# A gated-attention recurrence whose operands are prepared one chunk ahead in every round, instead of a lead that grows to two

## The chip, the cores and the metric

The kernel runs on one core of one Trainium2 chip. The metric is the device time of one execution in microseconds; the time before is 1066.51 us, the median of three runs.

## The reference, cut to what matters

Three stages follow each other: a gated linear attention over 4 batches of 768 tokens with 8 heads of 48, a mixture of 8 experts with the best two for each token, and a gated feed-forward layer with root-mean-square norm. The change lies in the first.

```
f = 1 / (1 + exp(-f_logit))
state = 0
for t in range(S):                       # 768 steps, every batch and head by itself
    state = f[t, :, None] * state + outer(k[t], v[t])
    y[t]  = q[t] @ state
x = y                                    # as (3072, 384)
noisy = x @ w_gate + log1p(exp(x @ w_noise)) * noise     # the router: two best of 8 experts
out += w * (relu(x[mask] @ w1[e]) @ w2[e])               # for each expert and each of the two
...                                                      # then norm, silu(gate) * val, w_out
```

## The kernel before

The recurrence is worked off in chunks of 128 tokens: 4 batches of 6 chunks, 24 chunks (numbers 0 to 23), all 8 heads of a chunk at once as 4 pairs in 128 partitions. With c the running sum of the gates' logarithms inside a chunk, the keys are scaled by exp(c) and the queries by exp(-c), so that a chunk needs only plain products.

What a chunk n passes through, by function:

- `clip` (L333, ACT): bounds the gate logits in place in `Fs`. `gates` (L343, ACT): two activations, exp and ln, into `L`, which has 2 buffers. `sums` (L351, DVE): a running sum over `L` into `cs`, which has 4 buffers; it is what frees a buffer of `L`.
- `prep` (L368): four steps. ACT makes `Ek` from `cs`, DVE the scaled keys `KT`, ACT turns `cs` over, DVE makes the scaled queries `QT` (and POOL copies a column to `hs`, for a check at the end). `KT` and `QT` have 3 buffers.
- `keys` (L387): PE transposes `KT`, ACT copies the result to `Ks`. The last chunk of a batch (5, 11, 17, 23) has no `keys` and no `state`.
- `scores` (L402): PE multiplies keys and queries; `masks` (L414, DVE) writes the masked product `AM`.
- `inter` (L447, PE): queries times the carried state, left out in the first chunk of a batch (0, 6, 12, 18). `state` (L421, PE) and `carry` (L433, DVE, tiles `su` and `Ss`) advance the state.
- `attend` (L458): PE adds `AM` times values, ACT copies the sum to `yT`. `rows` (L472): PE turns it into token rows and router logits, ACT copies out `x`, DVE reduces the logits to `lg`.

One round i of the loop in `gla_stream` (L1108) handles chunk i, finishes `rows` of chunk i-1 and prepares later chunks. The order of work on PE, ACT, DVE and POOL is written out: each of these engines executes its instructions in the order in which the program issues them, so that an instruction that waits holds up everything behind it on its engine. SP issues the plain loads and stores, in an order that a planner makes.

The lead before: `due(i, grows, lead)` (L1174) says which chunks a step of round i handles. Up to round `grows` it is chunk i+lead; in round `grows` two chunks at once; from then on chunk i+lead+1. Clips double in round 2, gates in round 3, sums in round 4, preps in round 5. From round 6 on the keys and queries of chunk i+2 are made in round i, and `keys(i+1)` stands right behind the first step of `prep`; in rounds 1 to 5 (`short`) it stands behind `inter(i)`. The loads of keys and queries (`load_kq_after`) and of gate logits (`load_f_after`) are issued behind the `prep` and `gates` of odd chunks, for the pair of chunks whose buffers these free.

Other work is spread over the rounds. `safe()` is called three times in a round (behind `scores`, behind `inter` and at the end) and each time takes one piece from the list `routing`: in rounds 12 to 19 the steps of the router for the first 12 chunks (mostly DVE, a few matmuls), from round 19 on the row gathers for the first expert blocks. In rounds 20 to 23 `take_part` splits a piece of expert weights into a high and a low part (ACT `whi`, DVE `wlo`), and in rounds 22 and 23 the first expert block's rows are transposed. After the loop the experts and the feed-forward layer follow as one stream of matmuls, again in an order written out for PE; the other engines' order is there made by the planner.

Of the kernel before, what the change touches and what calls it, by code (L numbers as in the profile page):

```python
# [27 lines left out]
def tile_gated_attention_moe_ffn(  # L28
# [23 lines left out]
    NT = B * NCH  # L52
# [100 lines left out]
    def bank(use, i=None):  # L153
        b = banks[0][use]
        if i is None:
            i = turns[use] = turns.get(use, -1) + 1
        k_ = b[i % len(b)]
        return (late["pp"] if k_ in "12" else pp).tile([P, 512], F32, name="bank" + k_)
# [141 lines left out]
    def load_f(n, count=2, cuts=WHOLE):  # L300
        b, src, dst = chunks_of(n, count)
        t = Fs[n // 2 % 3]
        for s in cuts:
            nc.sync.dma_start(t[:, s, dst], f_logit[b, s, :, src].rearrange("a d t -> d a t"))
        for k_ in range(count):
            _, _, at_ = chunks_of(n + k_, 1)
            st["f", n + k_] = t[:, :, at_]
# [13 lines left out]
    def load_f_after(n):  # L321
        if n % 2 and n + 5 < NT:
            load_f(n + 5)

    def load_kq_after(n):
        if n % 2 and n + 5 < NT:
            load_kq(n + 5)

    def run(fn, n, cuts=WHOLE):
        for _ in zip(*[fn(n, s) for s in cuts]):  # L330
            pass

    def clip(n, s=slice(0, HP), scalar=True):  # L333


        f = st["f", n][:, s]
        st["shift", n] = scalar
        if scalar:
            nc.scalar.activation(f, f, AF.Relu, bias=shift)
        else:  # L340
            nc.vector.tensor_scalar(f, f, -GATES_MAX - 1.5, None, op0=OP.max)

    def gates(n, s=slice(0, HP)):  # L343

        if s.start == 0:
            st["L", n] = wk.tile([P, HP, P], F32, name="L")
        f, l = st["f", n][:, s], st["L", n][:, s]
        nc.scalar.activation(l, f, AF.Exp, scale=-1.0, bias=shift if st["shift", n] else 0.0)
        nc.scalar.activation(l, l, AF.Ln, bias=1.0)

    def sums(n, s=slice(0, HP)):  # L351

        if s.start == 0:
            st["cs", n] = wk.tile([P, HP, P], F32, name="cs", bufs=4)
        nc.vector.tensor_tensor_scan(st["cs", n][:, s].rearrange("p a t -> p (a t)"),  # L355
                                     chain[:, s].rearrange("p a t -> p (a t)"),
                                     st["L", n][:, s].rearrange("p a t -> p (a t)"), 0.0,
                                     op0=OP.mult, op1=OP.add)
# [9 lines left out]
    def prep(n, s=slice(0, HP)):  # L368

        if s.start == 0:  # L370
            st["KT", n] = wk.tile([P, HP, P], F32, name="KT", bufs=3)
            st["QT", n] = wk.tile([P, HP, P], F32, name="QT", bufs=3)
            st["Ek", n] = wk.tile([P, HP, P], F32, name="Ek", bufs=1)
        cs, Ek = st["cs", n][:, s], st["Ek", n][:, s]
        nc.scalar.activation(Ek, cs, AF.Exp)
        yield
        nc.vector.scalar_tensor_tensor(st["KT", n][:, s], Ek, KEYS_MAX, st["kq", n][:, s, 0],
                                       op0=OP.min, op1=OP.mult)
        yield
        nc.scalar.activation(cs, cs, AF.Exp, scale=-1.0)  # L380
        yield
        nc.vector.tensor_tensor(st["QT", n][:, s], cs, st["kq", n][:, s, 1], op=OP.mult)
        if s.stop == HP:
            nc.gpsimd.tensor_copy(hs[:, n], st["cs", n][:, :, P - 1])
        yield

    def keys(n, copy=True):  # L387

        if n % NCH == NCH - 1:
            return  # L390
        p = cut(bank("K"), HP, P)
        for a in range(HP):
            flip(p[:, a, :], st["KT", n][:, a, :], ident)
        st["pK", n] = p
        if copy:
            keys_out(n)
# [711 lines left out]
    def gla_stream():  # L1108
        def valid(n):
            return 0 <= n < NT  # L1110

        with tc.manual_schedule(engines=ALL):
            rest = constants()
            load_f(0, 1, PARTS)
            next(rest)
            warm(10)
            load_kq(0, 1)
            load_f(1, 1)
            load_v(0)
            load_kq(1, 1)  # L1120
            load_f(2)
            load_kq(2)
            load_v(1)
            load_f(4)
            load_v(2)
            nc.sync.dma_start(columns[:, :, NX:], moe_w_both[:, :, :2 * E])
            load_kq(4)
            load_v(3)
            for t in Vs:
                nc.gpsimd.memset(t[:, DM:], 0.0)  # L1130
            for t in Ks + Ss:
                nc.gpsimd.memset(t[:, :, D:], 0.0)
            run(decay, 0, PARTS)
            halves = [prep(0, s) for s in PARTS]
            for _ in range(2):
                for half in halves:
                    next(half)
            clip(1, scalar=False)
            for _ in range(2):
                for half in halves:  # L1140
                    next(half)
            warm(3)
            keys(0, copy=False)
            gates(1)
            keys_out(0)
            scores(0, masked=False)
            sums(1)
            clip(2, scalar=False)
            masks(0)
            warm(2)  # L1150
            state(0)
            more = prep(1)
            next(more)
            next(more)
            next(rest)
            next(more)
            gates(2)
            next(more)
            carry(0)
            warm(5)  # L1160
            inter(0)
            attend(0)
            sums(2)
            keys(1)
            clip(3, scalar=False)
            gates(3)
            clip(4, scalar=False)
            next(rest)
            load_f_after(1)
            load_f_after(3)  # L1170
            load_kq_after(1)


            def due(i, grows, lead):  # L1174

                if i < grows:
                    ns = (i + lead,)
                elif i == grows:
                    ns = (i + lead, i + lead + 1)
                else:  # L1180
                    ns = (i + lead + 1,)
                return [n for n in ns if n < NT]

            for i in range(1, NT + 2):
                routing.extend(plan.get(i, []))
                if valid(i + 3):
                    load_v(i + 3)
                if valid(i):
                    scores(i)
                safe()  # L1190
                short = i < 6
                preps = due(i, 5, 1)
                more = prep(preps[0]) if preps else iter(())
                next(more, None)
                if valid(i + 1) and not short:
                    keys(i + 1)
                next(more, None)
                next(more, None)
                if valid(i - 1):
                    rows(i - 1)  # L1200
                for fn in turning.get(i, []):
                    fn()
                if valid(i):
                    inter(i)
                if valid(i + 1) and short:
                    keys(i + 1)
                safe()
                next(more, None)
                for n in preps[1:]:
                    run(prep, n)  # L1210
                for n in preps:
                    load_kq_after(n)
                if valid(i):
                    state(i)
                    carry(i)
                for n in due(i, 3, 3):
                    gates(n)
                    load_f_after(n)
                if valid(i):
                    attend(i)  # L1220
                for n in due(i, 4, 2):
                    sums(n)
                for n in due(i, 2, 4):
                    clip(n)
                safe()
                if i == 4:
                    nc.sync.dma_start(noise, moe_noise)
                    nc.sync.dma_start(gcol, moe2_rms_g)
                if i in (14, 16):
                    start_loads()  # L1230
                if i == 18:
                    nc.sync.dma_start(yd.rearrange("(e s) d -> s e d", e=E)[min(CAPS):],
                                      zeros[:, None, :].to_broadcast([SPAN - min(CAPS), E, DM]))
                if 20 <= i < 24:
                    take_part(0)
# [280 lines left out]
```

## Time and profile before

| what | value |
|---|---|
| time, median of 3 runs | 1066.51 us (1062.62 to 1069.57) |
| the profiled execution's own time | 1063.08 us |
| its span, first to last instruction | 1061.3 us |
| PE busy | 1027.7 us, 97% |
| DVE busy | 674.1 us, 64% |
| ACT busy | 486.1 us, 46% |
| POOL busy | 307.5 us, 29% |
| mean granted TensorE clock | 0.99 |

Busy shares are means over the whole span. The recurrence takes up its first part, some 150 us; in the rest PE hardly stops. A busy PE is not a PE at full clock: the granted clock stands in a column of its own.

### The profile page before, as it was taken

The numbers are of one execution on the slowest core, as the hardware profiler recorded it, in microseconds if no ns is written. First come the engines' busy times: TensorE is split into PE (matmuls) and PEld (weight loads), VectorE is DVE, ScalarE is ACT, GpSimd is POOL, SyncE is SP. The second block draws the span as 40 slices with busy tenths as digits, with TensorE's granted clock in tenths as the row PEclk, the third lists the DMA queues.
The fourth block names the chain that finished last, engine by engine and source line by source line (L and its number), as shares of the span: only waits on it lengthen the run. The fifth ranks groups of instructions, "written<-read, shape, count | busy, mean of one in ns | idle before, by whom it ended". The sixth has DMA issues, their size and how long they took to land.

```text
span 1061.3 us, 17487 instructions
## 1 busy us (share of the span) xinstructions
PE 1027.7 (97%) x6449; PEld 938.4 (88%) x6449; DVE 674.1 (64%) x1521; ACT 486.1 (46%) x1054; POOL 307.5 (29%) x350
## 2 busy tenths in 40 slices
PE   8998899999999999999999999999999999999996
PEld 5787789999999999999999988888888888888885
DVE  7698979878777757876665796354353354453332
ACT  6696655655555544655555543223232232232221
POOL 2000145545556655555550250110110200200000
PEclk9799999999999999999999999999999999999999
DMA  9975345666677756545555340110110200200000
GB/s 303 313 259 176 120 129 184 218 195 208 219 244 236 220 166 205 179 143 173 180 165 155 121 127 1 48 43 1 60 31 1 68 22 1 75 16 1 31 1 33
DMA packets 88946, 134.45 MB, mean 127 GB/s; under 512 B 8703, under 2 KB 64915, under 8 KB 88851
## 3 DMA queue, kind: packets, MB, share of 16 engines
q1 hardware_dynamic: 79475, 113.82, 32.7%
q0 software_dynamic: 9376, 19.43, 6.6%
q8 instruction: 52, 0.85, 0.3%
q14 instruction: 43, 0.35, 0.1%
HBM read 107.63 MB, written 25.59 MB: 126 GB/s over the span
## 4 chain that ended last, share of the span: by engine, by line
PE 77%; DVE 9%; DMA 7%; ACT 3%; issue 3%; SPq 1%; DVEq 0%; ACTq 0%
PE bank L681 68%; DMA raw<-in_moe_w_dram 5%; PE bank L173 2%; PE bank L476 2%; PE bank L454 2%; DVE wlo L210 1%; PE bank L464 1%; PE scores L408 1%; ACT whi L209 1%; DVE cs L355 1%; PE bank L725 1%; PE bank L728 1%; DVE AM L418 1%; PE bank L429 1%; DVE hh L816 1%
## 5 line engine op out<-in xcount | busy, mean ns | idle before, releaser
L681 PE MATMUL bank<-whi,hh 128*128 128x384 f32 x1360 | 379.7, 336 | 0.2 <-DVE y L843 0.2
L681 PE MATMUL bank<-xhi,whi 128*128 128x512 f32 (+8 forms) x816 | 303.3, 372 | 3.9 <-DVE hh L816 3.7
L681 PE MATMUL bank<-xhi,wlo 128*128 128x512 f32 (+8 forms) x816 | 301.3, 369 | 0.0
L681 PE MATMUL bank<-xlo,whi 128*128 128x512 f32 (+8 forms) x816 | 300.9, 369 | 0.0
L681 PEld LDWEIGHTS bank<-whi,hh 128*128 128x128 f32 x1360 | 248.5, 187 | 3.9 <-DVE y L843 0.6
L681 PE MATMUL bank<-wlo,hh 128*128 128x384 f32 x680 | 228.0, 335 | 0.0
L681 PEld LDWEIGHTS bank<-xhi,whi 128*128 128x128 f32 x816 | 153.3, 188 | 26.1 <-DVE hh L816 7.5
L681 PEld LDWEIGHTS bank<-xhi,wlo 128*128 128x128 f32 x816 | 153.2, 188 | 18.7 <-issue 0.2
L681 PEld LDWEIGHTS bank<-xlo,whi 128*128 128x128 f32 x816 | 153.3, 188 | 16.2
L210 DVE TENSOR_TENSOR wlo<-raw,whi 128x256 fp32r<-128x256 f32 (+1 forms) x320 | 143.1, 485 | 24.7 <-ACT whi L209 17.2
L209 ACT ACTIVATE whi<-raw 128x256 fp32r<-128x256 f32 (+1 forms) x320 | 126.2, 451 | 44.5 <-DMA raw<-in_moe_w_dram 33.0
L782 POOL DMA_INDIRECT xg<-xd,stokr x107 | 108.5, 1014 | 76.6 <-ACT hh L819 45.0
L681 PEld LDWEIGHTS bank<-wlo,hh 128*128 128x128 f32 x680 | 127.5, 187 | 3.3
L919 DVE TENSOR_TENSOR sg<-bank,sg 128x512 f32<-128x512 f32 x72 | 49.7, 691 | 120.2 <-ACT sg L918 120.2
L816 DVE SCALAR_TENSOR_TENSOR hh<-bank,hh 128x384 fp32r<-128x384 f32 (+7 forms) x176 | 76.4, 455 | 77.3 <-ACT hh L819 72.8
L870 POOL DMA_INDIRECT xg<-yd,slots x40 | 43.8, 1094 | 265.3 <-ACT hh L922 254.9
L782 POOL DMA_INDIRECT xg<-xd,stoka x84 | 90.3, 1075 | 89.9 <-ACT hh L819 56.9
L819 ACT ACTIVATE hh<-bank 128x384 fp32r<-128x384 f32 (+7 forms) x128 | 64.0, 500 | 103.0 <-PE bank L681 69.6
L918 ACT ACTIVATE sg<-bank 128x512 f32<-128x512 f32 x72 | 42.9, 596 | 143.3 <-PE bank L681 134.6
L922 ACT ACTIVATE hh<-sg 128x512 fp32r<-128x512 f32 x72 | 45.4, 630 | 123.7 <-DVE sg L920 123.6
L923 DVE TENSOR_TENSOR hh<-sg,hh 128x512 fp32r<-128x512 f32 x72 | 50.9, 706 | 46.8 <-ACT hh L922 46.8
L920 DVE TENSOR_TENSOR sg<-bank,sg 128x512 f32<-128x512 f32 x72 | 49.7, 691 | 40.2 <-PE bank L681 39.9
(172 smaller groups left out, 1003.2 us busy)
## 6 DMA issues: line engine op xcount, KB each, us to landing
raw<-in_moe_w_dram SPq DMA_DIRECT2D x64, 768.0 KB
Qs<-in_kq_dram SPq DMA_DIRECT2D x11, 1024.0 KB
yd<-y SPq DMA_DIRECT2D x48, 192.0 KB
Fs<-in_f_logit_dram SPq DMA_DIRECT2D x11, 512.0 KB
Vs<-in_v_dram SPq DMA_DIRECT2D x24, 192.0 KB
xd<-x SPq DMA_DIRECT2D x24, 192.0 KB
ya<-y SPq DMA_DIRECT2D x24, 192.0 KB
raw<-in_moe_w_gate_dram SPq DMA_DIRECT2D x6, 768.0 KB
```

The source lines that it names most:

```text
L209: nc.scalar.activation(hi[:, j], raw[:, j], AF.Copy)
L210: nc.vector.tensor_tensor(lo[:, j], raw[:, j], hi[:, j].bitcast(F32), op=OP.subtract)
L681: nc.tensor.matmul(o, a, b, start=start and i == 0, stop=stop and i == 2)
L782: paced(nc.gpsimd.indirect_dma_start(out=b.xg[i][:, k_], out_offset=None, in_=table, in_offset=bass.IndirectOffsetOnAxis(ap=rows_of[:, k_, ...
L816: return nc.vector.scalar_tensor_tensor(o, p[:, c], 0.0, hh[:, 0, c].bitcast(F32), op0=OP.max, op1=OP.subtract).ins
L819: mark[0] = nc.scalar.activation(hh[:, 0, :N], p[:, :N], AF.Relu).ins
L870: paced(nc.gpsimd.indirect_dma_start(out=y, out_offset=None, in_=ya if n < GROUP else yd, in_offset=bass.IndirectOffsetOnAxis(ap=at_, axis ...
L918: nc.scalar.activation(sg, ps[0], AF.Sigmoid)
L919: nc.vector.tensor_tensor(sg, ps[0], sg, op=OP.mult)
L920: nc.vector.tensor_tensor(sg, ps[1], sg, op=OP.mult)
L922: mark[0] = nc.scalar.activation(hh[:, 0], sg, AF.Copy).ins
L923: mark[1] = nc.vector.tensor_tensor(hh[:, 1], sg, hh[:, 0].bitcast(F32), op=OP.subtract).ins
```

## The change

The growing lead is taken out. `due` goes, and every round i prepares chunk i+1 (`prep`, `keys`), sums chunk i+2, takes the gates of chunk i+3 and clips chunk i+4. `keys(i+1)` stands behind `inter(i)` in all rounds. No computation is added or removed over the 24 chunks; it is dealt out to other rounds. Rounds 0 and 1 are as they were.

```
-            def due(i, grows, lead):
-                if i < grows:
-                    ns = (i + lead,)
-                elif i == grows:
-                    ns = (i + lead, i + lead + 1)
-                else:
-                    ns = (i + lead + 1,)
-                return [n for n in ns if n < NT]
-
             for i in range(1, NT + 2):
...
-                short = i < 6
-                preps = due(i, 5, 1)
-                more = prep(preps[0]) if preps else iter(())
+                more = prep(i + 1) if valid(i + 1) else iter(())
                 next(more, None)
-                if valid(i + 1) and not short:
-                    keys(i + 1)
                 next(more, None)
                 next(more, None)
                 if valid(i - 1):
                     rows(i - 1)
...
                 if valid(i):
                     inter(i)
-                if valid(i + 1) and short:
+                if valid(i + 1):
                     keys(i + 1)
                 safe()
                 next(more, None)
-                for n in preps[1:]:
-                    run(prep, n)
-                for n in preps:
-                    load_kq_after(n)
+                if valid(i + 1):
+                    load_kq_after(i + 1)
                 if valid(i):
                     state(i)
                     carry(i)
-                for n in due(i, 3, 3):
-                    gates(n)
-                    load_f_after(n)
+                if valid(i + 3):
+                    gates(i + 3)
+                    load_f_after(i + 3)
+                if valid(i + 4):
+                    clip(i + 4)
                 if valid(i):
                     attend(i)
-                for n in due(i, 4, 2):
-                    sums(n)
-                for n in due(i, 2, 4):
-                    clip(n)
+                if valid(i + 2):
+                    sums(i + 2)
                 safe()
```

## Rows read from the trace of the kernel before

**Rows 1.** Stretches: length; PE, PEld, DVE, ACT, POOL busy; granted clock, DMA share, GB/s.

```profile
16.00:21.40 5.40, 4.15 (x61) 3.56 (x62) 4.19 (x11) 3.92 (x8) 0.66 (x1) 1.00 1.11 345
36.10:49.90 13.80, 13.65 (x111) 11.48 (x109) 7.87 (x12) 6.88 (x14) 0.37 (x2) 0.51 0.92 326
64.60:69.70 5.10, 5.10 (x80) 4.53 (x78) 4.52 (x8) 4.30 (x8) 0.22 (x1) 1.00 0.64 211
97.60:101.10 3.50, 3.50 (x46) 3.15 (x43) 2.91 (x15) 2.29 (x5) 0.19 (x1) 0.52 0.16 59
```

**Rows 2.** Instructions in time around round 4: start, us, engine, idle before and releaser.

```profile
33.27 0.72 ACT L348 ACTIVATE L<-Fs,shift 128x512 f32<-128x512 f32 x1 [0.77 <-DVE cs L355]
34.56 0.58 ACT L469 ACTIVATE yT<-bank 128x512 f32<-128x512 f32 x1
35.19 1.15 PE L476 MATMUL bank<-columns,yT 128*128 128x112 f32 x8 [1.91 <-ACT yT L469]
```

**Rows 3.** The same view of round 2, PE and DVE: lead of one.

```profile
22.60 1.22 DVE L418 TENSOR_TENSOR AM<-scores,mask 128x1024 f32<-128x1024 f32 x1
23.75 0.68 DVE L377 SCALAR_TENSOR_TENSOR KT<-Ek,Qs 128x512 f32<-128x512 f32 x1
24.58 0.66 PE L173 MATMUL bank<-ident,KT 128*128 128x128 f32 x4
25.17 0.67 PE L429 MATMUL bank<-Vs,Ks 128*64 128x48 f32 x16
25.67 1.06 PE L464 MATMUL bank<-AM,Vs 128*64 128x128 f32 x16
25.89 0.36 DVE L442 TENSOR_TENSOR su<-bank,Ss 128x192 f32<-128x192 f32 x1 [0.70 <-PE bank L429]
27.87 1.23 DVE L418 TENSOR_TENSOR AM<-scores,mask 128x1024 f32<-128x1024 f32 x1
```

**Rows 4.** The same view, masks of rounds 6, 12, 14, 15, 17, 18, 20, 23.

```profile
51.69 1.20 DVE L418 TENSOR_TENSOR AM<-scores,mask 128x1024 f32<-128x1024 f32 x1
...
80.11 1.23 DVE L418 TENSOR_TENSOR AM<-scores,mask 128x1024 f32<-128x1024 f32 x1 [0.65 <-PE scores L408]
...
94.37 1.21 DVE L418 TENSOR_TENSOR AM<-scores,mask 128x1024 f32<-128x1024 f32 x1
...
103.00 1.20 DVE L418 TENSOR_TENSOR AM<-scores,mask 128x1024 f32<-128x1024 f32 x1
...
116.14 1.20 DVE L418 TENSOR_TENSOR AM<-scores,mask 128x1024 f32<-128x1024 f32 x1
...
122.05 1.20 DVE L418 TENSOR_TENSOR AM<-scores,mask 128x1024 f32<-128x1024 f32 x1
...
131.39 1.20 DVE L418 TENSOR_TENSOR AM<-scores,mask 128x1024 f32<-128x1024 f32 x1
...
146.83 1.22 DVE L418 TENSOR_TENSOR AM<-scores,mask 128x1024 f32<-128x1024 f32 x1
```

**Rows 5.** The same view, pieces of router and weight work inside the rounds.

```profile
97.28 0.20 PE L537 MATMUL bank<-r_both,before 128*128 128x96 bf16 x1 [3.94 <-DVE r_both L534]
98.35 0.26 DVE L544 COPY r_pos<-bank 128x104 f32<-128x104 f32 x1
110.68 1.22 DVE L575 TENSOR_TENSOR r_ol<-irowh,r_hf 128x1024 f16<-128x1024 f16 x1
113.01 0.69 DVE L377 SCALAR_TENSOR_TENSOR KT<-Ek,Qs 128x512 f32<-128x512 f32 x1
121.76 0.78 PE L585 MATMUL bank<-r_rh,r_ol 128*128 128x56 f16 x24
135.98 1.07 DVE L210 TENSOR_TENSOR wlo<-raw,whi 128x256 fp32r<-128x256 f32 x3
144.66 1.16 PE L408 MATMUL scores<-QT,KT 48*128 48x128 f32 x16
```

**Rows 6.** The same view, the first `rows` of the kernel.

```profile
17.25 1.12 PE L476 MATMUL bank<-columns,yT 128*128 128x112 f32 x8 [1.71 <-DMA columns<-in_moe_w_both_dram]
```

## The prediction

> **What bounds the kernel now.** Only the recurrence's order changes, so I read that part alone. The chain of waits shows PE in most rounds of its first half, then DVE in the rounds with the router, then PE again. From there I went to the granted clock by stretch, then to the instructions in order of time.
>
> The stretches show that the rounds in which the lead grows are the costly ones: from 36.10 to 49.90 us PE is busy for 13.65 of 13.80 us at a granted clock of 0.51, the lower of its two levels (1.2 instead of 2.4 GHz), while a later ordinary stretch runs at 1.00 [rows 1]. What PE did before it fell: it sat idle for 1.91 us in front of `rows(3)`, for `yT` on ACT, and `yT` stood behind the second `gates` of round 3, which itself waited for a running sum to free a buffer of `L` [rows 2]. So the doubled gates of round 3 made the gap, and the lower clock stretched rounds 4 and 5.
>
> Round 2 has the order that the change makes general. Its loop closes over DVE and PE: masks at 22.60, keys `KT` from 23.75 to 24.43, transposes at 24.58, state at 25.17, attend at 25.67, and the next masks at 27.87 behind the next scores [rows 3]. That is **5.27 us a round**: 1.83 from the masks to the end of `KT` and 3.44 from there to the next masks. PE has no slack in it, and DVE waits 0.70 us for the state [rows 3]. Whatever is put between masks and `KT` lengthens this loop in full. With the lead of two, `KT` and `QT` are a round old when PE wants them, and such work only fills DVE.
>
> **What goes.** Rounds 3 to 5 get the pattern of round 2. From the masks of round 3 (27.87, rows 3) to those of round 6 (51.69, rows 4) pass 23.82 us. With a lead of one, round 3 takes 5.27, round 4, without keys, 0.59 less (transposes to state, rows 3), 4.68, round 5, without state, 0.50 less (state to attend), 4.77: 14.72. **Gain 9.1 us.** Late next there would be ACT, which has one clip and one pair of gates a round as in round 2; I see nothing that brings the gap back. Its lower bound is 0, if a gap of the same kind opens elsewhere; its upper bound is the 9.1 itself.
>
> **What the shorter lead costs,** round by round, always from masks to masks.
>
> Rounds 6 to 11: before, 28.42 us [rows 4]. After, four rounds of 5.27 (round 6 has no `inter`, but PE must then wait for `KT`), 4.68 for round 10 and 4.77 for round 11: 30.53. **+2.1.**
>
> Rounds 12 and 13: before, 14.26 us [rows 4] with DVE filled by router work behind `inter` and at the round's end, not between masks and `KT`. That work covers the 0.70 us wait. I take 0, between 0 and +0.7 for each round.
>
> Round 14: before, 8.63 us [rows 4]. The router's matmuls start as soon as their input is there, at 97.28, and DVE goes on at 98.35 [rows 5]. After, the transposes of `KT` stand ahead of them on PE: 0.6 us at the full clock, 1.2 at the lower one, which PE has here anyway (0.52, rows 1). **+1.0.**
>
> Rounds 15 and 16: the router's step lies between masks and `KT` and takes 2.33 us (110.68 to 113.01, rows 5). Round 15 becomes 5.27 + 2.33 = 7.60. Round 16 has no keys, so DVE alone bounds it, as before; I give it 6.6. Sum 14.2 against 13.14 [rows 4]. **+1.1.**
>
> Round 17, without state: 4.77 + 2.33 = 7.10 against 5.91 [rows 4]. **+1.2.**
>
> Rounds 18 and 19: `KT` bounds round 18 (5.27) and the router's matmuls stand behind the transposes, 0.7 as an estimate, just under the 0.78 of their row [rows 5], since the next matmuls start into its end: 5.97. Round 19 has a small table step ahead of `KT`, 0.3 as an estimate from the smaller DVE rows: 5.57. Together 11.54 against 9.34 [rows 4]. **+2.2.**
>
> Rounds 20 to 22: before, 15.44 us [rows 4], the last of them with nothing left to prepare. After, rounds 20 and 21 have a full round's preparation and the weight split of 1.07 us at their end [rows 5], 6.3 each; round 22 has no keys and no sums, about 5.2: 17.8. **+2.3.** In round 23 some of this returns: before, the masks come 2.17 us behind the start of the scores (144.66 to 146.83, rows 5, 4), after only 1.2 (as 27.87 against the scores that end just ahead of it, an estimate). **-0.9.**
>
> Losses 2.1 + 0 + 1.0 + 1.1 + 1.2 + 2.2 + 2.3 - 0.9 = **9.0**, gain 9.1: the two cancel to 0.1 us.
>
> **Moved at no cost, and what covers it.** `hs` copies on POOL move a round later with `prep`, in front of a row gather from round 19 on; the gather is for expert blocks that start after the recurrence. The loads of keys, queries and gate logits are issued a round later, and used a round later; SP's queue holds them at the same distance from their use, and the transfers have room once the start is over (0.64 of the DMA time, rows 1). If that room is gone, `KT` waits, and by the loop above every such wait counts in full. The planner's order behind the recurrence may come out otherwise; ±1 us.
>
> **The unknown: the clock.** In rounds 15 and 17 the new order lets PE idle in one piece for about the 2.33 us between masks and `KT`; before, the same idle time lies in smaller pieces. The nearest rows: after 1.91 us the clock fell [rows 2, 1]; after 1.71 us [rows 6] the stretch stayed at 1.00 [rows 1]; after 3.94 us [rows 5] it was 0.52 for 3.5 us [rows 1]. So 2.33 lies on the side of a fall, though not far from the piece that did no harm. Price of one: between 3.5 x 0.48 = 1.7 us of lost PE work [rows 1] and 13.8 x 0.49 = 6.8 [rows 1], less what the DVE-bound rounds hide; below nothing it can't be, since a lower clock speeds nothing up. I take one fall at the near price, the one with the router's rounds around it: **+1.7.** In sum 0.1 + 1.7 = +1.8 us.
>
> The Trainium skill (TensorE: Matmul & The Clock Gate, Part 1) says that throttled is the default and sustained matmul activity releases it. By that rule every fall would cost one short release, 1.7 us here. The trace disagrees in one of its two cases: in rounds 4 and 5 nearly gapless matmuls ran through 13.8 us before the clock came back, so I keep 6.8 as the other end.
>
> **Rivals.**
>
> *The clock stays low through the router's rounds* (slower). Place: rounds 15 to 18, each with a gap for `KT`. Their PE work is 5.27 + 4.68 + 4.77 + 4.96 = 19.7 us (round 18 without `inter` and with the router's matmuls); at half clock that adds 19.7, of which the gaps hide 2.3 + 1.9 + 2.3 + 1.0 = 7.5. +12.2 us on the 0.1: about 1079. It decides once nearly all of these rounds run at the lower clock. For it: the 13.8 us stretch at 0.51 [rows 1]. Against it: the 3.5 us one, in just these rounds.
>
> *The gain stays* (faster). If the waits for `KT` in rounds 6 to 22 are half covered by DVE work that the loop lets run ahead, the losses are 4.5 and the time is 1066.5 - 4.6 = 1062; if none of them counted, 1057.4. For it: before, PE idles in these rounds too. Against it: round 2 has no slack on either engine [rows 3].
>
> *The low stretch only moves*: the new wait for `KT` in round 6, where no `inter` fills PE, is 1.0 us and could, with its neighbours, do what the 1.91 us did. Then 6.8 us of the gain are gone again: about 1074. Against it: 1.0 us is far below the 1.71 that did no harm.
>
> **How the numbers follow.** The profiled execution took 1063.08 us, 1.8 beside its span, and lies 3.4 below the median; I lay the sum on the median: 1066.51 + 1.8 = **1068**. Chances: forecast (1064 to 1072) 0.52; clock low through the router's rounds 0.17; the gain stays 0.22; the low stretch moves 0.09. The range 1060 to 1079 takes in the half-covered losses and most of the two slower cases. About 1% is what a measurement of this kernel tells from no change. Faster by that needs more than 10.6 us, above the whole gain: 0.04. Slower by it needs nearly all of the first rival: 0.14. Within: 0.82.
>
> **What would show each step.** In the profile after: granted clock 1.00 from 21 to 55 us and masks of round 6 near 42.6 us; rounds of 5.27 with DVE waiting 0.7 us for the state; idle PE in front of the key transposes of about 1.0 us in rounds 6 and 18 and 2.3 in rounds 15 and 17; the last scores within 2 us of 144.66. I am wrong if rounds 6 to 11 keep the pace of 28.4 us, if the clock falls somewhere in rounds 2 to 12, or if the expert stream behind the recurrence changes its length by more than 1 us.

## The result, and the profile after

The changed kernel takes 1070.97 us (median of 12 runs, 1066.69 to 1073.96); the kernel before, run beside it, 1063.45 (median of 12). The ratio is **1.0064, 95% interval 1.0041 to 1.0087**: 4.4 to 9.3 us slower, most likely 6.8. The forecast was 1068 with a range of 1060 to 1079, and 1.8 us more than before. The profiled execution took 1068.84 us, with a span of 1067.1.

The masks by round, in the same view as [rows 4]: those of rounds 6, 12, 14, 15, 17, 18, 20 and 23 of the changed kernel, and ahead of them round 3.

```profile
28.10 1.22 DVE L418 TENSOR_TENSOR AM<-scores,mask 128x1024 f32<-128x1024 f32 x1
...
43.72 1.23 DVE L418 TENSOR_TENSOR AM<-scores,mask 128x1024 f32<-128x1024 f32 x1 [1.11 <-PE scores L408]
...
76.11 1.23 DVE L418 TENSOR_TENSOR AM<-scores,mask 128x1024 f32<-128x1024 f32 x1 [1.11 <-PE scores L408]
...
90.99 1.21 DVE L418 TENSOR_TENSOR AM<-scores,mask 128x1024 f32<-128x1024 f32 x1
...
100.93 1.20 DVE L418 TENSOR_TENSOR AM<-scores,mask 128x1024 f32<-128x1024 f32 x1
...
116.38 1.20 DVE L418 TENSOR_TENSOR AM<-scores,mask 128x1024 f32<-128x1024 f32 x1
...
124.59 1.23 DVE L418 TENSOR_TENSOR AM<-scores,mask 128x1024 f32<-128x1024 f32 x1 [2.22 <-PE scores L408]
...
136.78 1.23 DVE L418 TENSOR_TENSOR AM<-scores,mask 128x1024 f32<-128x1024 f32 x1
...
154.84 1.22 DVE L418 TENSOR_TENSOR AM<-scores,mask 128x1024 f32<-128x1024 f32 x1
```

Differences of such rows make a table by stage. The predicted column holds the terms of the sum without the clock. The last three columns belong to experiments below: the clip put back, that and the idle time of PE filled, and the fastest version, which keeps the lead of two.

| rounds, masks to masks (us) | before | predicted | changed | clip_behind | both_mends | best_d |
|---|---|---|---|---|---|---|
| 3 to 5 | 23.82 | 14.72 | 15.62 | 14.74 | 14.74 | 18.36 |
| 6 to 11 | 28.42 | 30.53 | 32.39 | 30.65 | 30.65 | 28.41 |
| 12, 13 | 14.26 | 14.26 | 14.88 | 14.86 | 14.88 | 14.27 |
| 14 | 8.63 | 9.63 | 9.94 | 9.78 | 9.23 | 8.63 |
| 15, 16 | 13.14 | 14.20 | 15.45 | 15.64 | 14.07 | 13.15 |
| 17 | 5.91 | 7.10 | 8.21 | 8.03 | 7.00 | 5.91 |
| 18, 19 | 9.34 | 11.54 | 12.19 | 12.33 | 11.39 | 9.33 |
| 20 to 22 | 15.44 | 17.8 | 18.06 | 17.33 | 17.33 | 15.45 |
| sum | 118.96 | 119.78 | 126.74 | 123.36 | 119.29 | 113.51 |

Read the first line first: the gain in rounds 3 to 5 is there, 8.2 us. The stretches of the changed kernel, which answer to [rows 1]: length, the engines' busy time, granted clock, DMA.

```profile
21.00:55.00 34.00, 31.34 (x444) 26.49 (x438) 27.51 (x42) 28.02 (x51) 2.06 (x6) 1.00 1.06 364
94.60:97.90 3.30, 3.30 (x41) 3.22 (x43) 1.71 (x9) 2.21 (x4) 0.00 (x0) 0.50 0.17 61
104.80:108.90 4.10, 3.79 (x41) 3.29 (x43) 2.56 (x6) 2.56 (x5) 0.00 (x0) 0.59 0.02 3
121.90:128.70 6.80, 6.76 (x61) 5.83 (x57) 2.52 (x4) 4.83 (x9) 0.19 (x1) 0.51 0.18 59
```

The clock no longer falls at 36 us. It now falls three times in the rounds with the router, where the kernel before had one fall [rows 1]. What PE did before each: it waited for `KT`, as instructions in order of time show.

```profile
94.51 1.11 PE L173 MATMUL bank<-ident,KT 128*128 128x128 f32 x4 [2.86 <-DVE KT L377]
...
105.11 1.11 PE L173 MATMUL bank<-ident,KT 128*128 128x128 f32 x4 [2.49 <-DVE KT L377]
...
120.56 0.66 PE L173 MATMUL bank<-ident,KT 128*128 128x128 f32 x4 [2.49 <-DVE KT L377]
```

And an ordinary round takes 5.70 us, not the 5.27 of round 2 before. Round 8 of the changed kernel and the start of round 9, ACT and PE in order of time:

```profile
57.90 0.49 ACT L399 ACTIVATE Ks<-bank 128x384 f32<-128x384 f32 x1 [1.11 <-PE bank L173]
58.29 0.71 ACT L348 ACTIVATE L<-Fs,shift 128x512 f32<-128x512 f32 x1
...
59.03 0.63 ACT L349 ACTIVATE L<-L 128x512 f32<-128x512 f32 x1
...
59.57 0.71 ACT L339 ACTIVATE Fs<-Fs,shift 128x512 f32<-128x512 f32 x1
60.19 0.58 ACT L469 ACTIVATE yT<-bank 128x512 f32<-128x512 f32 x1
...
60.81 0.36 PE L476 MATMUL bank<-columns,yT 128*128 128x112 f32 x1 [0.36 <-ACT yT L469]
```

Here the clip (L339) runs ahead of the copy to `yT`. In the diff it is called in front of `attend`, where the kernel before called it behind `sums`. Round 2 before, ACT:

```profile
26.94 0.58 ACT L469 ACTIVATE yT<-bank 128x512 f32<-128x512 f32 x1
27.42 1.32 ACT L339 ACTIVATE Fs<-Fs,shift 128x512 f32<-128x512 f32 x2
```

With the clip in front, `yT` ends 0.36 us too late for PE, in every ordinary round, and the keys' copy `Ks` at the head of the chain waits for PE in turn.

### The profile page after: what moved, and what is told of

The parts are those of the page before. It is cut to its first block, busy times and chain, and to the rows that moved or that the text cites. A ratio compares the mean times of both kernels' runs of the same rounds, so it can differ in the third digit from the quotient of the medians.

```text
span 1067.1 us, 17480 instructions
## 1 busy us (share of the span) xinstructions
PE 1027.1 (96%) x6449; PEld 937.3 (88%) x6449; DVE 674.6 (63%) x1521; ACT 490.0 (46%) x1054; POOL 307.9 (29%) x350
## 4 chain that ended last, share of the span: by engine, by line
PE 83%; DVE 7%; ACT 5%; DMA 2%; issue 2%; SPq 1%; DVEq 0%; ACTq 0%
PE bank L681 74%; PE bank L173 2%; PE bank L476 2%; DMA raw<-in_moe_w_dram 2%; PE bank L454 1%; DVE wlo L210 1%; PE bank L728 1%; PE bank L725 1%; PE bank L464 1%; DVE AM L418 1%; ACT whi L209 1%; PE scores L408 1%; ACT L L349 1%; DMA columns<-in_moe_w_both_dram 1%; ACT L L348 1%
## 5 line engine op out<-in xcount | busy, mean ns | idle before, releaser
L870 POOL DMA_INDIRECT xg<-yd,slots x40 | 43.9, 1099 | 265.1 <-ACT hh L922 254.8
```

The source lines that it names most:

```text
L870: paced(nc.gpsimd.indirect_dma_start(out=y, out_offset=None, in_=ya if n < GROUP else yd, in_offset=bass.IndirectOffsetOnAxis(ap=at_, axis ...
```

## Experiments

Each was run against the kernel before on the same chip; ratios are to it.

**clip_behind: the clip back behind attend.**

```
-                if valid(i + 4):
-                    clip(i + 4)
                 if valid(i):
                     attend(i)
                 if valid(i + 2):
                     sums(i + 2)
+                if valid(i + 4):
+                    clip(i + 4)
```

> The changed kernel with clip(i + 4) put back behind attend and sums, where the kernel before has it. Theory: the changed order put the clip (0.71 us on ACT) ahead of the copy to yT, rows(i-1) waits 0.37 us for yT in every ordinary round, and a round takes 5.70 us instead of 5.27. Then rounds 7 to 9 fall to 5.27, the masks of round 6 come near 42.5 us (43.72 in the changed kernel), those of round 12 near 73.2 (76.11), and the time falls by some 3 us. Rival: the copy to Ks, which waits 1.1 us for the transposed keys and stands ahead of both gates, holds up yT by itself; then the rounds stay at 5.6 to 5.7 and the time is within 1 us of the changed kernel.

Ratio 1.0033 (1.0012 to 1.0054), about half of the change's loss. ACT and PE of round 8, in order of time:

```profile
55.99 0.49 ACT L399 ACTIVATE Ks<-bank 128x384 f32<-128x384 f32 x1 [0.85 <-PE bank L173]
...
57.66 0.58 ACT L469 ACTIVATE yT<-bank 128x512 f32<-128x512 f32 x1
58.14 0.71 ACT L339 ACTIVATE Fs<-Fs,shift 128x512 f32<-128x512 f32 x1
```

```profile
52.11 1.16 PE L408 MATMUL scores<-QT,KT 48*128 48x128 f32 x16
...
57.38 1.16 PE L408 MATMUL scores<-QT,KT 48*128 48x128 f32 x16
58.47 1.15 PE L476 MATMUL bank<-columns,yT 128*128 128x112 f32 x8
```

From scores to scores pass 5.27 us, and `rows` waits for nothing. `Ks` still waits 0.85 us for the keys; so it was not `Ks` that held up `yT`. The rival falls. In the table the clip accounts for 126.74 - 123.36 = 3.4 us (3.0 where PE's idle time is filled in both: warm_fill, below, has 122.32, both_mends 119.29).

What is left of the loss in ordinary rounds is not a wait. A stretch of one round here, and one of the kernel before, each from scores to scores:

```profile
52.11:57.38 5.27, 5.27 (x79) 4.53 (x77) 4.50 (x8) 4.36 (x9) 0.37 (x1) 1.00 0.66 222
59.48:64.55 5.07, 5.07 (x79) 4.50 (x77) 4.73 (x9) 4.43 (x9) 0.19 (x1) 1.00 0.91 277
```

PE is busy throughout in both. With `keys` behind `inter` instead of behind `scores`, the same matmuls take 0.2 us more; why they do is not shown.

**warm_fill: PE kept busy where it waited for `KT`.** `warm(n)` issues n matmuls on ones that nobody reads.

```
                 if valid(i):
                     inter(i)
+                if i in (14, 15, 17):
+                    warm(12 if i == 14 else 10)
                 if valid(i + 1):
                     keys(i + 1)
```

> The changed kernel with matmuls on ones, whose results nobody reads, put on PE between inter and keys in rounds 14 (12 of them), 15 and 17 (10 each), where PE sat idle 2.86, 2.49 and 2.49 us. Theory: these gaps let the granted clock fall three times (94.6 to 97.9, 104.9 to 108.9, 121.9 to 128.7 us), and the slow transposes, state and attend behind each lengthen the loop. Then the clock is 1.00 through rounds 14 to 18, round 15 takes 7.6 instead of 8.85, round 17 7.1 instead of 8.21, round 18 6.0 instead of 6.80, and the time falls by 3 to 4 us. Rival: VectorE bounds these rounds and hides the lower clock; then the clock is 1.00 and the time falls by less than 1 us.

Ratio 1.0033 (1.0014 to 1.0053): the other half. The clock from 26 to 150 us, one stretch:

```profile
26.00:150.00 124.00, 111.34 (x1530) 91.57 (x1526) 104.31 (x213) 88.33 (x164) 15.58 (x27) 1.00 0.61 198
```

From 26 us on not one fall is left. Round 17 took 7.00 us (masks at 115.89 and 122.89), rounds 14 to 19 together 41.69 where the changed kernel took 45.79. So DVE did not hide the lower clock, although it is DVE that PE waits for: behind the late `KT` come the transposes, state, attend and scores, all on PE, and the next masks wait for the last of them.

**both_mends.** Both edits at once.

> The changed kernel with both mends at once: the clip behind attend and sums, and the matmuls on ones in rounds 14, 15 and 17. Theory: the two losses are separate (each mend alone moved the ratio to the kernel before from 1.0064 to 1.0033), so together they bring it to 1.000, between 0.998 and 1.002; masks of rounds 3 and 23 some 118.8 us apart (126.7 in the changed kernel). What is then left against the kernel before is the short lead by itself: its gain in rounds 3 to 5 against the waits for KT. Rival: both mends touch the same waits in the rounds with the router, and together give hardly more than one; then the ratio stays at 1.002 or above.

Ratio 1.0027 (1.0007 to 1.0047), hardly below either mend alone, which is what the rival said. The profile says otherwise: the recurrence has both savings, 119.29 us from round 3 to round 23, and no fall in it. What the profiled execution had instead was a fall before that, in rounds 1 and 2 (0.69 over 15 to 26 us), where PE waits some 1.7 us for a load, as in [rows 6]. The whole column stands within 0.5 us of my working, 119.78. The clocks of the single runs fit a loss that only some of them have: the six fastest of 12, with mean clocks of 0.996 to 0.998, took 1059.6 to 1060.8 us, close to the 1060.43 of before; the five below 0.995 took 1062.7 to 1067.9. lead_one_best, below, takes up the fall in round 1.

**clip_front: the clip's place alone, in the kernel before.**

```
+                for n in due(i, 2, 4):
+                    clip(n)
                 if valid(i):
                     attend(i)
                 for n in due(i, 4, 2):
                     sums(n)
-                for n in due(i, 2, 4):
-                    clip(n)
```

> The kernel before, with its lead of two, and the clip put ahead of attend as the changed kernel has it: one part of the change alone. Theory: with a lead of two ACT copies the keys early, so the chain from rows over x, both gates and the clip to yT ends about with attend, and the clip's place costs nothing; the masks of rounds 6 and 12 stay 28.4 us apart and the time stays within 1.5 us of the kernel before. Rival: the clip ahead of yT costs 0.4 us in each ordinary round whatever the lead; then the time is 4 to 6 us above the kernel before.

Ratio 1.0046 (1.0027 to 1.0066). The size is the rival's, the place is neither's. Rounds 6 to 11 take 29.03 us (masks at 55.13 and 84.16), 0.6 more than before; rounds 3 to 5 take 26.79, 3.0 more. There the clip lengthened the gap that was there already and opened a second one:

```profile
37.12 2.05 PE L476 MATMUL bank<-columns,yT 128*128 128x112 f32 x8 [2.52 <-ACT yT L469]
46.59 2.05 PE L476 MATMUL bank<-columns,yT 128*128 128x112 f32 x8 [1.97 <-ACT yT L469]
```

The 0.6 us of rounds 6 to 11 came in round 6, from whose scores to the next 4.94 us pass (before 4.31). From the scores of round 8 to those of round 10 pass 10.14 us in both kernels (63.52 to 73.66, before 59.48 to 69.62). So with a lead of two the clip's place costs an ordinary round nothing, as the theory had it; with a lead of one it costs 0.43. The rival's size came from the rounds in which the lead grows; another 0.6 us came in rounds 20 to 22 (16.04), and their cause is open.

**gates_behind: the kernel before, without its gap in round 4.** In round 3 the second `gates`, in round 4 the only one, stand behind `attend`.

```
-                for n in due(i, 3, 3):
+                late_gates = due(i, 3, 3)
+                if i not in (3, 4): ...          # gates and load_f_after for all, as before
+                elif i == 3: ...                 # for the first alone
                 if valid(i):
                     attend(i)
+                if i in (3, 4): ...              # for those left over
```

> The kernel before, with its lead of two, but in round 3 the second pair of gates and in round 4 the gates stand behind attend, so that the copy to yT no longer stands behind them on ACT. Theory: the 1.91 us gap of round 4 and with it the 13.8 us at a clock of 0.51 come from that order alone; then the clock is 1.00 from 21 to 55 us, the masks of round 6 come 6 to 8 us ahead of 51.69, and the time is some 7 us below the kernel before. Rival: the doubled sums of round 4 (2.4 us on DVE ahead of the masks of round 5) make a gap of 1.5 us ahead of the transposes in round 5 in its place and the clock falls there; then less than 3 us are gained.

Ratio 0.9968 (0.9951 to 0.9985): 3.4 us gained, not 7. The clock stayed up through rounds 4 and 5, but PE was busy for only 10.44 of 14.00 us there:

```profile
36.00:50.00 14.00, 10.44 (x142) 8.66 (x138) 10.85 (x16) 10.94 (x20) 1.09 (x3) 1.00 1.00 337
```

```profile
40.85 1.16 PE L408 MATMUL scores<-QT,KT 48*128 48x128 f32 x16 [1.02 <-DVE QT L382]
...
45.83 0.66 PE L173 MATMUL bank<-ident,KT 128*128 128x128 f32 x4 [1.72 <-DVE KT L377]
```

The theory is right about the cause of the fall, the rival about what is late next: the doubled sums and preps themselves. Rounds 3 to 5 took 19.21 us (masks at 30.82 and 50.03). Ahead of them this profile had lost 3.0 us (masks of round 3 at 30.82, before at 27.87) in a fall in rounds 1 and 2, shown at the end.

**l_three: a third buffer of `L` in the kernel before,** `bufs=3` in `gates`, nothing else.

> The kernel before with three buffers of L instead of two, nothing else. Theory: of the 1.91 us gap in round 4, 0.77 us was the wait of the second gates for a buffer and 1.35 their own time ahead of yT; without the wait the gap is about 1.1 us and the clock stays at 1.00 through rounds 4 and 5; then the masks of round 6 come at 45 to 47 us instead of 51.69 and the time is 4 to 6 us below the kernel before. Rival: the gates of round 4 or the doubled sums still open gaps above 1.5 us there and the clock falls in most executions; then less than 2 us are gained.

Ratio 0.9972 (0.9954 to 0.9991), 2.9 us. The gap is 1.03 us where 1.1 was expected, the clock 1.00, and the masks of round 6 come at 46.66:

```profile
34.74 1.15 PE L476 MATMUL bank<-columns,yT 128*128 128x112 f32 x8 [1.03 <-ACT yT L469]
```

```profile
36.00:50.00 14.00, 12.25 (x180) 10.46 (x180) 11.88 (x19) 11.65 (x22) 1.27 (x4) 1.00 1.05 369
```

The mechanism holds in this profile, which is that of the fastest of the 12 runs (1054.08 us): the masks of round 6 come 5.0 us earlier. Between the medians less than the 4 to 6 us came; why is not shown.

**best_a: gates_behind and 16 matmuls on ones in round 14.**

> The kernel before with the late gates of rounds 3 and 4 behind attend, and 16 matmuls on ones on PE in round 14, where it sat idle 3.94 us and the clock fell for 3.5 us. Theory: the clock is 1.00 in round 14, the 1.7 us of PE work lost there come back in part, since DVE bounds the round: 0.5 to 1.5 us below gates_behind (ratio 0.9968). Rival: DVE hides all of it; then the ratio is that of gates_behind within 0.0005.

Ratio 0.9975 (0.9959 to 0.9992), as gates_behind. The clock was 1.00 in round 14, and round 14 took 8.63 us all the same (masks at 91.80 and 100.43). So with a lead of two the lower clock costs nothing there; that DVE hides it because no transposes stand between is argued, not tested. This profile has falls at other places, from 43.9 to 50.6 and from 146.3 to 149.6 us. The first is the fall that the rival of gates_behind named, behind the same wait in round 5:

```profile
43.04 0.65 PE L173 MATMUL bank<-ident,KT 128*128 128x128 f32 x4 [1.73 <-DVE KT L377]
```

In the profile of gates_behind the clock stayed up behind 1.72 us; here it did not, and rounds 6 to 11 took 30.16 us instead of 28.42.

**best_d: the same with a third buffer of `L` and 8 matmuls on ones in round 1.**

> As best_a, with three buffers of L and 8 matmuls on ones in round 1, where PE waits some 1.7 us for a load and the clock fell in the profile of gates_behind (17 to 24 us) but not in that of the kernel before. Theory: the late gates no longer wait for a buffer, Ek and KT of rounds 4 and 5 come about 0.8 us earlier each, and no execution loses the clock in rounds 1 and 2 (2 to 3 us where it did): 1 to 4 us below best_a, with a smaller spread between runs. Rival: the gaps of rounds 4 and 5 come from DVE's doubled sums and preps, not from ACT, and the extra matmuls of round 1 delay rows(0); then it is no faster than best_a.

Ratio **0.9947 (0.9929 to 0.9965)**, 1054.06 us, with runs from 1052.6 to 1055.76: faster than both kernels. In its profile the clock stayed up from 8 us to the recurrence's end, in one stretch:

```profile
8.00:150.00 142.00, 128.95 (x1771) 108.92 (x1772) 121.62 (x247) 102.77 (x197) 23.18 (x50) 1.00 0.70 225
```

From round 3 to round 23 l_three alone took 113.49 us in its profile, best_d 113.51: there the late gates and the matmuls of round 14 brought nothing beyond the third buffer.

**lead_one_best: both_mends and the 8 matmuls of round 1,** the lead of one with all that helped.

> The changed kernel with the clip behind attend, matmuls on ones in rounds 14, 15 and 17, and 8 more in round 1: the lead of one with every mend that best_d has for the lead of two. Theory: the fall of the clock in round 1 was what held both_mends at 1.0027; without it the ratio is 0.999 to 1.001, the clock 1.00 throughout the recurrence and the masks of rounds 3 and 23 are 119.3 us apart, against 113.5 in best_d: the lead alone is worth 5 to 6 us. Rival: the short lead leaves runs with falls elsewhere (rounds 12, 20) and the ratio stays at 1.002 or above.

Ratio 1.0005 (0.9992 to 1.0019), as expected, though the clock of the profiled execution, the slowest of the twelve (1067.99 us), was not 1.00 throughout: it fell at 9.2 to 12.5 us and again between 97.0 and 101.9, and rounds 3 to 22 took 120.59 us. Ten of the twelve runs have a mean clock of 0.996 to 0.998 and took 1061.6 to 1064.3 us. Between the ratio and that of best_d, taken on another chip beside other runs of before, lie 0.0058, some 6 us: about that is what the lead of two, with its `keys` behind `scores`, is worth once little else hinders either kernel, and the table has it as 119.29 - 113.51 = 5.8.

**before_warm1: the kernel before with the 8 matmuls of round 1 alone.**

> The kernel before with 8 matmuls on ones in round 1 alone. Theory: it removes only the falls in round 1 (2 to 3 us in the executions that have one) and leaves the gap of round 4: the ratio is 0.998 to 1.000 and the clock still falls at about 36 us. Rival: the execution with a fall in round 1 and the one in round 4 exclude each other, since the later one only comes when PE ran at full clock before; then the ratio is 1.000 to 1.002.

Ratio 0.9976 (0.9961 to 0.9991), a little more than expected. The gap of round 4 is there (1.90 us), but this time the low clock after it was short: 0.88 over 36 to 50 us, against 0.51 in [rows 1], and round 6's masks came at 49.00. How much of the gain is round 1's and how much that luck, one profile does not say. The rival, 1.000 to 1.002, falls.

## Why the prediction was right, and where not

**The gain** was 8.2 us against 9.1. The doubled gates made the gap, the gap the low clock (gates_behind, l_three). The missing 0.9 is the clip again: round 3 took 5.70 instead of 5.27 and round 4 5.12 instead of 4.68 (14.74 together with round 5 with the clip put back, 14.72 predicted). The low clock and the gap are not all of the gain: without them the growing lead still takes 18.36 us for these rounds (best_d), so 5.5 of the 9.1 us are theirs and 3.6 the growing lead's own.

**The step that failed** is "Late next there would be ACT, which has one clip and one pair of gates a round as in round 2; I see nothing that brings the gap back". Round 2 before has two clips, and they stand behind `yT`. The diff moves the call in front of `attend`; I counted how often ACT's work is done and not what stands behind it. It cost 3.4 us from round 3 on. Nor did round 1 stay as it was: its clip moved too (at 21.47, ahead of `yT` at 22.09; before at 22.06, behind `yT` at 21.59), and round 2 took 5.61 us instead of 5.27.

**The short lead itself**, rounds 6 to 22: predicted 105.06 us, measured without clip and falls (both_mends) 104.55. The loop of round 2, with the router's 2.33 us put into it, gives each stage to within 0.7 us. The account behind it holds in part. PE waits 0.80 us for `KT` in rounds 6 and 18 (about 1.0 was named), and without the extra matmuls 2.49 in rounds 15 and 17. In rounds 7 to 10 it waits for nothing: there 5.27 us is PE's own work, in the order with `keys` behind `inter`, and not a loop over `KT`. The number was right because it was read from a round with that order.

**The clock** was one fall at 1.7 us in the sum; there were two more than before, and filling all three places was worth 123.36 - 119.29 = 4.1 us. The side was right (2.49 us of idle time, above the 1.91 that had done it), the count and the price were low. The 1.71 us "that did no harm" was chance: the same wait was followed by a fall in three other profiles (last section). The Trainium skill (TensorE: Matmul & The Clock Gate, Part 1) says that sustained activity ends a fall. Here the three lasted 3.3, 3.4 (0.59 over 4.1 us) and 6.8 us with PE busy for nearly all of each; read as one short release for every fall, as in the prediction, that agrees with two of them, and no single price holds.

**Round 23** was to give back 0.9 us. It gave nothing: from its masks to the last `rows` 5.28 us passed before and 5.51 after. The masks came 1.90 us behind the start of the scores (152.94 to 154.84), not 1.2, and the way from the scores to the last `rows` stayed the same, 7.45 us before and 7.41 after.

**The sum against the profiles.** Round 3 to round 23 went up by 7.8 us, the predicted sum of these stages by 0.8 without the clock. Clip (3.4) and clock (4.1) make the difference, less 0.5 by which the short lead cost less than predicted. The sum itself has a slip of sign: losses of 9.0 less a gain of 9.1 are -0.1, not +0.1, so the forecast should have been 0.2 us lower. The spans differ by only 5.8: the expert stream behind the recurrence took 909.2 us in the profile of before (152.11 to the end) and 906.75 after. In eight other profiles it took 905 to 906, with either lead, but 909.5 in before_warm1 and 911.5 in lead_one_best. So it differs between executions, and whether the change has a part in the 2.4 us is not shown. The prediction had named more than 1 us here as a sign of being wrong. Two more of its signs failed: the masks of round 6 came at 43.72 and not near 42.6 (42.68 with the clip put back), and the last scores at 152.94, 8.3 us behind 144.66 where 2 were allowed.

Of the rivals, the low clock through the router's rounds came half true: falls in rounds 14, 15, 17 and 18, not in all of them. That it stayed within 1% was right, at 0.64%. That 1068 came as near to 1070.97 as it did is in part luck: it was laid on 1066.51, the median of three runs, and the kernel before has 1063.45 over the twelve. The 1.8 us that the sum gave lie below the measured 4.4 to 9.3; the range, from 6.5 us below its base to 12.5 above, holds them.

## What to carry to other kernels

When a step moves in a written order, list for each engine what now stands behind it and who waits for that; their number alone did not tell it here. A lead pays by what it lets lie between producer and consumer: with one chunk, each piece put between masks and `KT` lengthened the round nearly in full (7.47 and 7.00 us in rounds 15 and 17, where 7.60 and 7.10 would be all of it), with two it filled idle time. Growing a lead in midstream has its price too (18.36 against 14.74 us for three rounds at full clock), so nothing that PE waits for should stand behind the doubled work.

## What the runs showed of the hardware

The same gap does not always cost the same. In round 1 PE waits 1.71 to 1.76 us for a load in six of the profiles without the extra matmuls there. In three (before, the changed kernel, clip_behind) the clock stayed at 1.00 from 15 to 26 us; in warm_fill it was 0.84, in gates_behind and both_mends 0.69:

```profile
17.00:24.00 7.00, 6.89 (x56) 6.07 (x58) 3.28 (x7) 3.06 (x6) 0.66 (x1) 0.51 1.10 351
```

That stretch is of gates_behind. Once down, the clock stayed there for anything from 3.3 to 13.8 us, with PE busy. Nor does the kernel before lose its clock alike in every execution: of the 30 runs beside best_d seven have a mean clock of 0.994 and took 1057.4 to 1058.3 us; the other 23 have 0.991 or less, with a median of 1060.9. Matmuls on ones, whose results are thrown away, in the idle time kept it up in each place where I put them, but one: in lead_one_best it was down already when those of round 15 came. There it fell behind 1.63 us of idle time ahead of that round's scores, where I had put none; both_mends has the same 1.63 us there, and no fall. The version whose profile shows no fall in the recurrence from 8 us on, best_d, also had the narrowest spread of times, 3.2 us, but over 7 runs only; the 30 runs of before beside it spread over 7.1.
